# Strided and local attention into a gated two-layer MLP on one core: a planner with outstanding transfers, re-measured step lengths, and output weights behind the first attention units

## The chip, the cores and the metric

The kernel runs on one core of one Trainium2 chip. The time is device microseconds of one execution. The kernel before was timed in three runs: 538.31, 539.55 and 541.49 us, median 539.55. One more execution, 537.99 us long, was taken with a profile; all rows of the trace come from it.

## What is computed

Eight batches of eight heads, 576 tokens each, head width 64. The first four heads see a local window of 32 tokens, the other four see the tokens of their own residue modulo 32. The attention output, 4608 tokens by 512, goes through a first product with `w_in` (512 by 1024), a softmax gate, a layer norm with gain `g_ln`, and a second product with `w_out` (1024 by 512).

```python
scores = scale * np.matmul(q, k.transpose(0, 1, 3, 2))
mask_local = (rel >= 0) & (rel < stride)
mask_strided = (rel >= 0) & (pos[None, :] % stride == pos[:, None] % stride)
...
attn = attn / (np.sum(attn, axis=-1, keepdims=True) + 1e-09)
x = np.ascontiguousarray(attn_out.transpose(0, 2, 1, 3)).reshape(B * S, H * D)
h = x @ w_in
solu = h * softmax(h)
ln = (solu - mu) / np.sqrt(var + 1e-06) * g_ln
return (ln @ w_out).astype(np.float32)
```

(`softmax` stands here for the four lines of the reference that write it out.)

## The kernel before

**Two kinds of work.** An attention *unit* is a part of a batch: units 0 and 1 of a batch are the strided heads (12 and 10 blocks of 54), units 2, 3 and 4 the local heads (6 times 2 blocks of 96, three blocks of 64 queries each). There are 40 units. A *tile* is 128 tokens of the MLP; there are 36, and `ff(n)` writes tile n.

**A unit** (function `unit`) multiplies q and k on PE into `s_ps` (lines 381 and 386), takes the maximum and subtracts it on DVE (392, 393), the exponential on ACT (395), the sum and its reciprocal on DVE (396, 400, 401), the product with the reciprocal on POOL (404), splits the result into two fp16 parts on ACT (410) and DVE (411), and transposes them by DMA from SP (413). PE then multiplies with v into `x_ps` (434), and ACT (450) and DVE (451) split the result into the ring `xhi`, `xlo`. A strided unit uses both banks of `x_ps`, so the next unit's product waits for lines 450 and 451. The v of a batch is scaled and split (343), and copies of it are moved within the core by DMA (line 357: four into `vd` for the strided heads, three into `ve` for the local ones); line 434 waits for these moves as well.

**A tile** has a first product of two halves, 12 matmuls of 128x512 each, into two of the three banks of `h_ps` (492 to 494), a maximum on DVE (499, 500), exp on ACT (501), the gated product on DVE (503, 506), a square on ACT (507), small norms on POOL (511 to 545), the fp16 split on ACT (552) and DVE (553), one transpose by DMA (556; for the last two tiles four smaller ones, 560), the second product of two halves, 12 matmuls each (565 to 567), and a store from ACT (573 and the DMA behind it). The banks rotate, so the first half of tile n+1 goes into a bank that tile n doesn't use, and its second half waits for line 503 of tile n.

**The weights.** `w_in` (four loads of 1 MB) and `w_out` (four loads of 1 MB) come as 64-bit floats and are decoded by ACT (593) and DVE (596, 597). For `w_in` follow squares on ACT (606), a sum on PE (284), a power-of-two scale on DVE (290 to 296), and the split into two parts (611 on ACT, 612 on DVE). For `w_out` follow squares (622), eight matmuls of fp32 (632) with a matrix of gains that POOL writes (627), a scale, and the folding of gain and mean into the weights (641, 645, 647, 648). The sum of the squares of `w_out` uses a bank of `h_ps` that the first product of tile 0 needs.

**What sets the order.** Nothing is scheduled at run time. Each step is given to a `Plan` with its engine, a length, what it reads and writes, and for some a due time: `G1[n]` for the first product of tile n, `G2[n]` for its second, `PV[n]` for a unit's product with v. `dues` hands due times back from a step to those that it depends on, with a slack factor for each engine. `order` then plays the program through, always taking, on the engine that is free first, the ready step with the earliest due time, and the kernel is written out in that order. Each engine runs its instructions in that order and waits where a result is missing. The order of steps on the same buffers is that in which they were given to the plan. In `Plan` before, a DMA takes a fixed latency of 5.34 on top of its length, and a transpose from SP is a DMA like any other.

**The DMA queue.** SP issues nearly all DMAs, in order; the stores come from ACT. Eight semaphores are handed out in turn to the DMAs, so a DMA isn't issued before the eighth DMA ahead of it has landed.

Of the kernel before, what the change touches and what calls it, by code (L numbers as in the profile page):

```python
# [18 lines left out]
STRIDE = 32  # L19
# [41 lines left out]
class Plan:  # L61

    DMA_LATENCY = 5.34
    DMA_AHEAD = 1.0
    HOP = 0.50
    SLACK = {"pe": 0.89, "act": 1.59, "dve": 1.94, "pool": 0.82, "sp": 0.80}
    LOAD_LEAD = 6.88  # L70

    def __init__(self):
        self.steps = []
        self.dma = {}
        self.loads = set()
        self.writer, self.readers = {}, {}

    def add(self, eng, dur, fn, key, r=(), w=(), lock=None, dma=None):
        n = len(self.steps)
        if dma:  # L80
            self.dma[n] = dma
# [14 lines left out]
        self.steps.append((eng, dur, fn, key, deps, lock))  # L96

    def dues(self):
        steps = self.steps
        due = self.due = [float("inf") if s[3] is None else s[3] for s in steps]  # L100
        for m in range(len(steps) - 1, -1, -1):
            for d in steps[m][4]:
                e, dur = steps[d][:2]
                need = due[m] - dur * self.SLACK[e] - self.HOP
                if e == "sp":
                    need -= self.DMA_LATENCY
                if d in self.dma:
                    need -= self.dma[d] + self.DMA_LATENCY
                if not steps[d][4] or d in self.loads:
                    need -= self.LOAD_LEAD  # L110
                due[d] = min(due[d], need)

    def order(self):
        steps = self.steps
        self.dues()
        key = self.due
# [8 lines left out]
        dma_free = 0.0  # L125
# [5 lines left out]
        while len(out) < len(steps):  # L131
            best = None
            for e, ns in waiting.items():
# [3 lines left out]
                n = min((n for n in ns if ready_at[n] <= now), key=lambda n: (key[n], n))  # L137
# [6 lines left out]
            if e == "sp":  # L144
                dma_free = max(dma_free, now + 0.55) + dur
                free[e] = max(now + 0.55, dma_free - self.DMA_AHEAD)
                end = dma_free + self.DMA_LATENCY
            elif n in self.dma:
                free[e] = now + dur
                dma_free = max(dma_free, free[e]) + self.dma[n]  # L150
                end = dma_free + self.DMA_LATENCY
            else:
                if steps[n][5]:
                    now = max(now, locked["pool" if e == "dve" else "dve"])
                    locked[e] = now + dur
                free[e] = end = now + dur
# [10 lines left out]
def attn_solu_kernel(ctx: ExitStack, tc: tile.TileContext, qloc, qstr, kloc, kstr, vloc, vstr, w_in, w_out, g, masks, out):  # L167
# [107 lines left out]
    def pow2_scale(dst, parts, r, w, room, top=14, mul=1.0, square=None):  # L275
# [24 lines left out]
        add("dve", 0.2, root, None, r=[T], w=[(w, "root")])  # L300
        add("dve", 0.5, fn, None, r=[(w, "root")], w=[w])
# [5 lines left out]
    def load_qk(b, half):  # L307
        w = 2 * (S, SP)[half]
        k0 = 0 if half else KPAD
        load(1.65, q_raw[half][:, 0:w], (qloc, qstr)[half][b], [("q", half)])  # L310
        load(1.65, k_raw[half][:, k0 : k0 + w], (kloc, kstr)[half][b], [("k", half)])


    def load_v(b, a):
        w = [("vr", a, raw_v(b))] + ([("room", i) for i in range(4)] + [("half", i) for i in range(8)] if b == 2 else [])
        load((1.8, 2.2)[a], vr_sb[raw_v(b)][a], (vloc, vstr)[a][b], w)

    def v_scale(b):
# [43 lines left out]
    def unit(n):  # L362
# [29 lines left out]
        add("dve", w + 0.13, lambda: nc.vector.tensor_reduce(mx.rearrange("p (c x) -> p c x", c=2), sv, axis=AX.X, op=ALU.max), None, r=SS, w=[M])
        add("dve", w + 0.13, lambda: nc.vector.tensor_tensor(t4, sv, mx.rearrange("p (c x) -> p c x", c=2).unsqueeze(3).broadcast_to([P, 2, nb, nk]), op=ALU.subtract),
            None, r=[*SS, M], w=[T])
        add("act", nx * nk / 1200 + 0.19, lambda: nc.scalar.activation(tv, tv, AF.Exp, scale=0.125), None, r=[T], w=[T])
        add("dve", w + 0.1, lambda: nc.vector.tensor_reduce(sm, tv, axis=AX.X, op=ALU.add), None, r=[T], w=[M])
# [7 lines left out]
        add("pool", nx * nk / 500 + 0.1, lambda: nc.gpsimd.tensor_tensor(tv, tv, sm.unsqueeze(2).broadcast_to([P, nx, nk]), op=ALU.mult),  # L404
# [6 lines left out]
        add("dve", w + 0.1, lambda: nc.vector.tensor_tensor(lo, tv, hi, op=ALU.subtract), None, r=[T, PB], w=[PB], lock=True)  # L411
        nt = nx if half else 2 * nx
        add("sp", 0.16 * nt, lambda: nc.sync.dma_start_transpose(ptb[:, 0:nt], pb[:, 0:nt].rearrange("p a k -> p (a k)")), None, r=[PB], w=[PT])
# [24 lines left out]
        add("pe", nx * (0.063 if half else 0.095) + 0.1, pv, PV[n], r=[PT, *VR], w=X)  # L438
# [16 lines left out]
    def ff(n):  # L455
# [21 lines left out]
        else:  # L477
# [8 lines left out]
            add("dve", 0.3, cross, None, r=[(x, b % 4) for b in bs for x in ("hsc", "osc")], w=SC, lock=True)  # L486
# [12 lines left out]
        add("dve", 1.21, lambda: nc.vector.tensor_reduce(nm, hv, axis=AX.XY, op=ALU.max, negate=True), None, r=HH, w=[(ST, "nm")])  # L499
# [3 lines left out]
        add("dve", 1.3, lambda: nc.vector.scalar_tensor_tensor(uv, hv, 1.0, ev, op0=ALU.mult, op1=ALU.mult, accum_out=us), None,  # L503
# [3 lines left out]
        add("act", 1.35, lambda: nc.scalar.activation(e, u, AF.Square, bias=mean, scale=Q, accum_out=sq), None,  # L507
# [6 lines left out]
        if n < EARLY:  # L514
# [6 lines left out]
            add("pool", 1.0, first, None, r=[(ST, "mean"), (ST, "sq"), "nhalf"], w=[(ST, "r")], lock=False)  # L521
# [223 lines left out]
```

## Time and profile before

| | |
|---|---|
| median of three runs (lowest to highest) | 539.55 us (538.31 to 541.49) |
| profiled execution: its time, and the span of its trace | 537.99 us, 536.3 us |
| busy time of PE, DVE, ACT, POOL | 473.2, 363.0, 298.4, 172.1 us |
| mean granted clock of TensorE | 0.978 |

The page gives for each engine the time in which it ran an instruction. A row of the timeline has the start, the length, the engine, the line, the operation with its tiles and shapes, and, in brackets, how long the engine had been idle and what let it go. A row of the windows has a stretch of the span, and for PE, PEld, DVE, ACT and POOL the busy time and number of instructions in it, then the granted TensorE clock, the mean busy share of the 16 DMA engines (sums over queues can pass 1) and GB/s. A row of the waits has the total, the count and the longest.

### The profile page before, as it was taken

How to read it: one execution, taken by the hardware profiler on the slowest of the kernel's cores; microseconds unless marked ns; L12 is line 12 of the kernel's file. 1: busy time of each engine (PE TensorE's matmuls, PEld its weight loads, DVE VectorE, ACT ScalarE, POOL GpSimd, SP SyncE). 2: the span in 40 equal slices, each digit the busy share in tenths (PEclk: the TensorE clock that was granted, in tenths of full speed). 3: DMA queues.
4: the chain of work that ended last, by engine and by line, in shares of the span. 5: the costliest groups of instructions: out<-in, count | busy, mean ns of one | idle time of the engine just before them, and what ended most of it. 6: DMA issues, size and time to landing. Idle time of an engine off the chain costs nothing.

```text
span 536.3 us, 11679 instructions
## 1 busy us (share of the span) xinstructions
PE 473.2 (88%) x4780; PEld 242.5 (45%) x4780; DVE 363.0 (68%) x627; ACT 298.4 (56%) x432; POOL 172.1 (32%) x314
## 2 busy tenths in 40 slices
PE   2027848899999999998999999999999999999994
PEld 2013524445454555554545454455555454444441
DVE  2977896779676767685767676796667766645440
ACT  3857563487566556654665557555456554543541
POOL 3123005265232443332443222233234423321220
PEclk9998888799999999999999999999999999999999
DMA  8999884999995999599956995699746974443332
GB/s 343 370 223 355 169 227 121 168 147 274 258 215 101 279 193 213 119 195 257 223 111 180 198 255 111 125 240 195 165 90 141 224 160 89 90 88 78 81 85 72
DMA packets 155349, 96.89 MB, mean 181 GB/s; under 512 B 138272, under 2 KB 138912, under 8 KB 154784
## 3 DMA queue, kind: packets, MB, share of 16 engines
q1 hardware_dynamic: 150112, 86.71, 74.0%
q10 hardware_dynamic: 5184, 9.44, 5.3%
q8 instruction: 37, 0.61, 0.5%
q14 instruction: 16, 0.13, 0.1%
HBM read 39.24 MB, written 9.44 MB: 91 GB/s over the span
## 4 chain that ended last, share of the span: by engine, by line
PE 73%; DMA 13%; DVE 7%; POOL 2%; issue 2%; ACT 2%; SPq 1%; ACTq 0%; POOLq 0%; DVEq 0%
PE h_ps L492 10%; PE o_ps L565 10%; PE h_ps L493 10%; PE h_ps L494 10%; PE o_ps L567 10%; PE o_ps L566 10%; DMA cc<-cc 7%; PE x_ps L434 5%; PE s_ps L386 4%; DMA raw<-w_out 3%; DMA pt<-p 2%; DMA vrs<-vstr 1%; PE s_ps L381 1%; PE o_ps L632 1%; DVE st L499 1%
## 5 line engine op out<-in xcount | busy, mean ns | idle before, releaser
L492 PE MATMUL h_ps<-w,xhi 128*128 128x512 f16 x280 | 108.0, 386 | 1.3 <-DVE raw L503 1.2
L493 PE MATMUL h_ps<-w,xhi 128*128 128x512 f16 x280 | 107.9, 385 | 0.0
L494 PE MATMUL h_ps<-w,xlo 128*128 128x512 f16 x280 | 107.8, 385 | 0.0
L565 PE MATMUL o_ps<-obuf,cc 128*128 128x512 f16 x272 | 103.4, 380 | 3.6 <-DMA cc<-cc 3.6
L566 PE MATMUL o_ps<-obuf,cc 128*128 128x512 f16 x272 | 103.1, 379 | 0.0
L567 PE MATMUL o_ps<-obuf,cc 128*128 128x512 f16 x272 | 103.1, 379 | 0.0
L404 POOL TENSOR_TENSOR t<-t,m 128x576 f32<-128x576 f32 (+2 forms) x40 | 54.7, 1368 | 92.8 <-DVE m L401 34.9
L499 DVE TENSOR_REDUCE st<-h_ps 128x1 f32<-128x1024 f32 x35 | 42.7, 1221 | 53.4 <-PE h_ps L494 51.8
L533 POOL TENSOR_SCALAR st<-st 128x1 f32<-128x1 f32 x32 | 10.5, 327 | 175.5 <-DVE st L506 175.1
L553 DVE SCALAR_TENSOR_TENSOR cc<-raw,st,cc 128x1024 f16<-128x1024 f32 (+1 forms) x38 | 48.9, 1290 | 17.5 <-ACT cc L552 17.5
L501 ACT ACTIVATE raw<-h_ps,st,vsc 128x1024 f32<-128x1024 f32 x31 | 37.3, 1203 | 39.5 <-DVE st L500 39.1
L552 ACT ACTIVATE cc<-raw,st 128x1024 f16<-128x1024 f32 (+1 forms) x38 | 41.6, 1100 | 23.9 <-POOL st L542 19.7
L507 ACT ACTIVATE raw<-raw,st 128x1024 f32<-128x1024 f32 x36 | 41.3, 1147 | 18.8 <-DVE st L506 12.9
L411 DVE TENSOR_TENSOR p<-t,p 128x576 f16<-128x576 f32 (+2 forms) x40 | 30.4, 759 | 25.2 <-ACT p L410 25.2
L503 DVE SCALAR_TENSOR_TENSOR raw<-h_ps,raw 128x1024 f32<-128x1024 f32 x35 | 42.5, 1215 | 6.3 <-ACT raw L501 6.3
L567 PEld LDWEIGHTS <-cc 128*128 128x128 f16 x288 | 28.1, 98 | 37.1 <-DMA cc<-cc 3.2
L565 PEld LDWEIGHTS <-cc 128*128 128x128 f16 x288 | 28.1, 97 | 36.7 <-DMA cc<-cc 4.9
L494 PEld LDWEIGHTS <-xlo 128*128 128x128 f16 x288 | 28.5, 99 | 35.1 <-issue 1.9
L493 PEld LDWEIGHTS <-xhi 128*128 128x128 f16 x288 | 28.5, 99 | 34.4 <-issue 3.4
L492 PEld LDWEIGHTS <-xhi 128*128 128x128 f16 x288 | 28.5, 99 | 34.0 <-issue 1.9
L386 PE MATMUL s_ps<-k,q 64*54 64x54 f32 (+1 forms) x1280 | 41.8, 274 | 1.8 <-DMA k<-kstr 1.8
L573 ACT ACTIVATE ob<-o_ps,st 128x512 f32<-128x512 f32 x34 | 23.3, 684 | 35.3 <-PE o_ps L567 30.8
(130 smaller groups left out, 727.2 us busy)
## 6 DMA issues: line engine op xcount, KB each, us to landing
out<-ob ACTq DMA_DIRECT2D x36, 256.0 KB, 3.1
vd<-vs SPq DMA_DIRECT2D x16, 384.0 KB, 6.2
q<-qstr SPq DMA_DIRECT2D x8, 594.0 KB, 4.6
k<-kstr SPq DMA_DIRECT2D x8, 594.0 KB, 5.6
q<-qloc SPq DMA_DIRECT2D x8, 576.0 KB, 5.2
k<-kloc SPq DMA_DIRECT2D x8, 576.0 KB, 6.5
raw<-w_in SPq DMA_DIRECT2D x4, 1024.0 KB, 12.5
vrs<-vstr SPq DMA_DIRECT2D x5, 768.0 KB, 7.8
```

The lines of the kernel that those rows point to most:

```text
L386: nc.tensor.matmul(s_ps[row : row + nq, pair, i * nk : (i + 1) * nk], q_raw[half][hs, q0 : q0 + (nq - 1) * nqb + 1 : nqb], k_raw[half][hs, ...
L404: add("pool", nx * nk / 500 + 0.1, lambda: nc.gpsimd.tensor_tensor(tv, tv, sm.unsqueeze(2).broadcast_to([P, nx, nk]), op=ALU.mult), None, ...
L492: nc.tensor.matmul(hv[:, i], xhi[:, cc, tok], whi[:, cc, cols], start=(cc == 0), stop=False)
L493: nc.tensor.matmul(hv[:, i], xhi[:, cc, tok], wlo[:, cc, cols], start=False, stop=False)
L494: nc.tensor.matmul(hv[:, i], xlo[:, cc, tok], whi[:, cc, cols], start=False, stop=(cc == 3))
L499: add("dve", 1.21, lambda: nc.vector.tensor_reduce(nm, hv, axis=AX.XY, op=ALU.max, negate=True), None, r=HH, w=[(ST, "nm")])
L503: add("dve", 1.3, lambda: nc.vector.scalar_tensor_tensor(uv, hv, 1.0, ev, op0=ALU.mult, op1=ALU.mult, accum_out=us), None, r=[*HH, E], w=[ ...
L552: add("act", w / 1020 + 0.15, lambda cols=cols: nc.scalar.mul(c[:, 0, cols], u[:, cols], r), None, r=[U, (ST, "r")], w=CC[0][mine])
L553: add("dve", w / 880 + 0.15, lambda cols=cols: nc.vector.scalar_tensor_tensor(c[:, 1, cols], u[:, cols], r, c[:, 0, cols], op0=ALU.mult, o ...
L565: nc.tensor.matmul(o, ct[:, cc, :], ohi[:, cc, :], start=(cc == 0), stop=False)
L566: nc.tensor.matmul(o, ct[:, cc, :], olo[:, cc, :], start=False, stop=False)
L567: nc.tensor.matmul(o, ct[:, 8 + cc, :], ohi[:, cc, :], start=False, stop=(cc == 7))
```

## The change

It changes the planner, its numbers, and the place of two groups of steps. No instruction is added or removed, and none changes its shape.

- The planner knows eight outstanding transfers (`lanes`), a landing time (`LAND`, `LATE`), and for each SP step how long the issuing engine is held (`issue=(took, hold)`): a transpose holds SP until shortly before it lands. Locks between DVE and POOL are applied to all steps.
- Nearly all step lengths, the slack factors and the due times have new numbers. `LAG`, the planned distance between a tile's first and second product, went from 31.30, 34.52, 17.64 (first tile, seventh tile, last tile) to 33.36, 47.73, 50.87.
- The first piece of `w_out` depends on the writer of the second transpose buffer (`("pt", 1)`). As the piece is given to the plan behind units 0 to 4, that writer is the transpose of unit 3.
- `prep_o()` (everything on `w_out`) is given to the plan behind the units of batch 0, not ahead of them; the factor that needs its result is a function of its own, `o_factor`.

```diff
-FIRST = 3.59
-STEP = 12.74
-LEAD = 18.32
-LAG = [31.30, 34.52, 17.64]
+FIRST = -1.35
+STEP = 12.91
+LEAD = 17.42
+LAG = [33.36, 47.73, 50.87]
...
-    DMA_LATENCY = 5.34
-    DMA_AHEAD = 1.0
-    HOP = 0.50
-    SLACK = {"pe": 0.89, "act": 1.59, "dve": 1.94, "pool": 0.82, "sp": 0.80}
-    LOAD_LEAD = 6.88
+    LAND = 2.3
+    LANES = 8
+    HOP = 0.21
+    LATE = 0.59
+    SLACK = {"pe": 1.49, "act": 1.44, "dve": 1.24, "pool": 2.53, "sp": 4.64}
+    LOAD_LEAD = 4.91
...
+            if steps[n][5]:
+                now = max(now, locked["pool" if e == "dve" else "dve"])
+                locked[e] = now + dur
+            if n in self.issue:
+                took, hold = self.issue[n]
+                if e != "sp":
+                    now += dur
+                now = max(now, lanes[lane])
+                dma_free = max(now + 0.8, dma_free) + (dur if e == "sp" else 0.5)
+                landed = lanes[lane] = dma_free + self.LAND - 0.8
+                lane = (lane + 1) % self.LANES
+                free[e] = now + took if hold is None else max(now + took, landed - hold)
+                end = landed + self.LATE
...
+    def o_factor(b):
+        sc = vsc_sb[b % 4]
         add("dve", 0.2, lambda: nc.vector.tensor_scalar(sc[:, 3:4], sc[:, 4:5], ...
...
-        add("sp", 0.16 * nt, lambda: nc.sync.dma_start_transpose(...), None, r=[PB], w=[PT])
+        add("sp", 0.142 * nt, lambda: nc.sync.dma_start_transpose(...), None, r=[PB], w=[PT], issue=(1.0, 3.5))
...
-        load(2.9, room, src, RAW)
+        load(2.61, room, src, RAW, [("pt", 1)] if n == 4 else [])
...
     prep_w()
-    prep_o()
...
+            if b:
+                o_factor(b + 1)
         unit(b * NU + NU - 1)
+        if b == 0:
+            prep_o()
+            o_factor(0)
+            o_factor(1)
```

What this makes of the order is shown here on three engines. In these rows the number behind `m`, `t` and `p` counts the buffer: in batch 0, `m0` to `m4` belong to units 0 to 4, and `p0`, `p1`, `p2`, `p0`, `p1` to units 0 to 4 in turn. Line numbers of the changed kernel are 4 lower in `unit`, `ff` and the weights (6 lower in the first functions).

DVE at the start, around the scale of `w_in` (`w_sc`), before:

```order
L343 SCALAR_TENSOR_TENSOR vl0_71<-vrl0_69,vsc0_77,vl0_71 128x1280
L596 TENSOR_SCALAR raw0_67<-raw0_67 128x1024
L597 SCALAR_TENSOR_TENSOR obuf0_113<-obuf0_113,raw0_67 128x1024
L396 TENSOR_REDUCE m1_90<-t1_86 128x10
L290 TENSOR_SCALAR w_sc0_114<-h_ps_119 128x1
```

and now:

```order
L592 TENSOR_SCALAR raw0_67<-raw0_67 128x1024
L593 SCALAR_TENSOR_TENSOR cc0_101<-cc0_101,raw0_67 128x1024
L447 TENSOR_TENSOR xlo0_100<-x_ps_120,xhi0_99 128x2x18x18
L407 TENSOR_TENSOR p0_94<-t3_88,p0_94 128x6x96
L339 SCALAR_TENSOR_TENSOR vl0_71<-vrl0_69,vsc0_77,vl0_71 128x1280
L284 TENSOR_SCALAR w_sc0_114<-h_ps_119 128x1
```

Ahead of the scale stood the decoding of the first piece of `w_out` (into `obuf`) and unit 1's sum; now the result of unit 0 (`xlo`, line 447) and unit 3's split stand there, and the decoding of `w_out` has moved behind.

SP at the start (`raw` and `cc` are loads of weights, `q1`, `k1`, `vr` loads of batch 1, `vd` and `ve` moves of v, `pt` the transposes), before:

```order
L305 DMA raw0_67<-w_out 128x2x1024
L357 DMA vd0_74<-vs0_72 64x2x1536 x2
L357 DMA vd0_74<-vs0_72 64x1536 x2
L305 DMA vrs0_70<-vstr 128x1536
L657 DMA g0_116<-g 128x8
L305 DMA q10_64<-qstr 128x1188
L413 DMA_TRANSPOSE pt0_97<-p0_94 128x12x128
L305 DMA vrl0_69<-vloc 128x1280
L305 DMA raw0_67<-w_out 128x2x1024 x2
```

and now:

```order
L299 DMA q10_64<-qstr 128x1188
L299 DMA k10_66<-kstr 128x1188
L409 DMA_TRANSPOSE pt0_97<-p0_94 128x12x128
L353 DMA vd0_74<-vs0_72 64x2x1536 x2
L409 DMA_TRANSPOSE pt1_98<-p1_95 128x10x128
L353 DMA vd0_74<-vs0_72 64x1536 x2
L299 DMA vrs0_70<-vstr 128x1536
L299 DMA raw0_67<-w_out 128x2x1024
L409 DMA_TRANSPOSE pt1_98<-p0_94 128x12x128
```

Unit 0's transpose had one piece of `w_out` and the four moves into `vd` ahead of it; now it has neither, and two of the moves stand behind unit 1's transpose.

ACT at the end (a row of 569 or 573 is the store of a tile; `st0` to `st3` are tiles 32 to 35 here, and the row that reads `x_ps` is the exponential of the last tile), before:

```order
L501 ACTIVATE raw0_67,st3_107<-x_ps_120,st3_107,vsc3_80 128x1024
L507 ACTIVATE raw0_67,st3_107<-raw0_67,st3_107 128x1024
L573 ACTIVATE ob1_103<-o_ps_121,st1_105 128x512
L574 DMA out<-ob1_103 128x512
L552 ACTIVATE cc0_101<-raw0_67,st3_107 128x512 x2
L573 ACTIVATE ob0_102<-s_ps_118,st2_106 128x512
L574 DMA out<-ob0_102 128x512
L573 ACTIVATE ob1_103<-s_ps_118,st3_107 128x512
```

and now:

```order
L497 ACTIVATE raw0_67,st3_107<-x_ps_120,st3_107,vsc3_80 128x1024
L503 ACTIVATE raw0_67,st3_107<-raw0_67,st3_107 128x1024
L569 ACTIVATE ob0_102<-o_ps_121,st0_104 128x512
L570 DMA out<-ob0_102 128x512
L548 ACTIVATE cc0_101<-raw0_67,st3_107 128x512 x2
L569 ACTIVATE ob0_102<-s_ps_118,st2_106 128x512
L570 DMA out<-ob0_102 128x512
L569 ACTIVATE ob1_103<-o_ps_121,st1_105 128x512
L570 DMA out<-ob1_103 128x512
L569 ACTIVATE ob1_103<-s_ps_118,st3_107 128x512
```

Behind the exponential of the last tile stood the stores of tiles 33, 34 and 35; now those of 32, 34, 33 and 35 stand there.

More of the change, by code (lines that the diff above doesn't have):

```diff
@@ L95, in add @@
         lock = eng == "pool" if lock is None else lock
-        self.steps.append((eng, dur, fn, key, deps, lock))
+        self.steps.append((eng, dur, fn, due, deps, lock))
+        if issue or eng == "sp":
+            self.issue[n] = issue or (0.45, None)
     def dues(self):
@@ L115, in order @@
         self.dues()
-        key = self.due
+        due = self.due
         left = [len(s[4]) for s in steps]
@@ L136, in order @@
                 now = max(free[e], min(ready_at[n] for n in ns))
-                n = min((n for n in ns if ready_at[n] <= now), key=lambda n: (key[n], n))
+                n = min((n for n in ns if ready_at[n] <= now), key=lambda n: (due[n], n))
                 if best is None or now < best[0]:
@@ L254, in load_masks @@
     def load_masks():
-        add("sp", 0.6, lambda: nc.sync.dma_start(mask_sb, masks), None, w=["mask_raw"])
-        add("pool", 1.5, masks_bf16, None, r=["mask_raw"], w=["mask"])
+        add("sp", 0.4, lambda: nc.sync.dma_start(mask_sb, masks), None, w=["mask_raw"])
+        add("pool", 1.34, masks_bf16, None, r=["mask_raw"], w=["mask"])
     for i in range(NPB):
@@ L348, in v_split @@
             moves = (
-                (1.3, ve_sb[0:D], v_sb[0][D:P]),
-                (0.5, ve_sb[D:KL, :, 0:last], v_sb[0][0:STRIDE, :, cd:]),
-                (0.1, ve_sb[D:KL, :, last:], v_sb[0][0:STRIDE, :, 0:cd]),
-            )
-        else:
-            moves = [(1.2, vd_sb[0:D, :, y], v_sb[1][y * D : y * D + D]) for y in range(2)]
-            moves += [(0.6, vd_sb[D:P, 0, y], v_sb[1][y * D : y * D + D, 0]) for y in range(2)]
+                (1.0, ve_sb[0:D], v_sb[0][D:P]),
+                (0.4, ve_sb[D:KL, :, 0:last], v_sb[0][0:STRIDE, :, cd:]),
+                (0.2, ve_sb[D:KL, :, last:], v_sb[0][0:STRIDE, :, 0:cd]),
+            )
+        else:
+            moves = [(1.0, vd_sb[0:D, :, y], v_sb[1][y * D : y * D + D]) for y in range(2)]
+            moves += [(0.4, vd_sb[D:P, 0, y], v_sb[1][y * D : y * D + D, 0]) for y in range(2)]
         for i, (dur, dst, src) in enumerate(moves):
@@ L519, in first @@
                 nc.gpsimd.tensor_tensor(r, v, nhalf, op=ALU.pow)
-            add("pool", 1.0, first, None, r=[(ST, "mean"), (ST, "sq"), "nhalf"], w=[(ST, "r")], lock=False)
+            add("pool", 1.9, first, None, r=[(ST, "mean"), (ST, "sq"), "nhalf"], w=[(ST, "r")], lock=False)
             def second():
@@ L569, in ff @@
         for i in range(2):
-            add("pe", 2.6, lambda i=i: g2(i), G2[n], r=[(*CT, i, 0), (*CT, i, 1), *(("o_w", cc) for cc in range(4 * i, 4 * i + 4))], w=[O])
+            add("pe", 2.62, lambda i=i: g2(i), G2[n], r=[(*CT, i, 0), (*CT, i, 1), *(("o_w", cc) for cc in range(4 * i, 4 * i + 4))], w=[O])
         def store():
@@ L627, in gains @@
             nc.gpsimd.tensor_scalar(gmat, g_sb.unsqueeze(2).broadcast_to([P, 8, P]), -1.0 / DF, None, op0=ALU.mult)
-        add("pool", 2.3, gains, None, r=["g"], w=["gmat"])
+        add("pool", 2.8, gains, None, r=["g"], w=["gmat"])
         for cc in range(8):
-            add("pe", 0.87, lambda cc=cc: nc.tensor.matmul(o_ps, gmat[:, cc], obuf[:, cc], start=(cc == 0), stop=(cc == 7)), None,
+            add("pe", 1.0, lambda cc=cc: nc.tensor.matmul(o_ps, gmat[:, cc], obuf[:, cc], start=(cc == 0), stop=(cc == 7)), None,
                 r=["gmat", ("od", cc)], w=["o"])
```

118 lines of the change are left out of this document (50 added, 68 removed).

## The prediction

> **What bounds the kernel now.** I read the page first, then windows that cut the span where PE changes its pace, then the timelines of PE and DVE at the start and at the end. The page has PE busy for most of the span, and its slices show where it isn't: in the first seven and in the last.
>
> ```profile
> PE 473.2 (88%) x4780; PEld 242.5 (45%) x4780; DVE 363.0 (68%) x627; ACT 298.4 (56%) x432; POOL 172.1 (32%) x314
> ...
> PE   2027848899999999998999999999999999999994
> ...
> PEclk9998888799999999999999999999999999999999
> ```
>
> The windows put numbers on it (first number after the stretch: its length; next: PE busy; third of the busy times: DVE).
>
> ```profile
> 0.00:20.00 20.00, 3.72 (x98) 3.03 (x98) 9.48 (x18) 11.26 (x12) 7.56 (x18) 1.00 0.91 367
> 20.00:40.00 20.00, 3.03 (x60) 2.42 (x60) 16.21 (x26) 13.63 (x21) 2.49 (x1) 1.00 1.08 256
> 40.00:60.00 20.00, 14.13 (x182) 7.64 (x183) 16.97 (x25) 13.86 (x26) 4.90 (x4) 0.87 1.10 318
> 60.00:80.00 20.00, 11.96 (x174) 6.78 (x176) 17.37 (x35) 11.29 (x18) 2.42 (x2) 0.84 0.80 182
> 80.00:97.70 17.70, 13.77 (x167) 7.57 (x161) 13.04 (x24) 7.28 (x10) 6.78 (x4) 0.79 0.57 116
> 97.70:134.00 36.30, 35.12 (x361) 17.90 (x361) 29.36 (x58) 24.49 (x36) 19.39 (x33) 0.93 0.97 209
> 134.00:500.00 366.00, 362.27 (x3620) 184.39 (x3619) 251.00 (x433) 203.67 (x292) 121.42 (x234) 1.00 0.80 169
> 500.00:536.30 36.30, 29.15 (x134) 12.78 (x132) 9.59 (x15) 12.93 (x20) 7.11 (x20) 1.00 0.32 80
> ```
>
> PE's idle time is length less busy time: 16.3 + 17.0 + 5.9 + 8.0 + 3.9 = 51.1 us up to 97.7, 1.2 us from there to 134, 3.7 us in the long middle, 7.2 us at the end. From 97.7 to 500 PE is the bound at 99%, and an order can gain there at most those 4.9 us. The change must pay at the start and at the end. At the start DVE is busy for 64 us of the 77.7 from 20 to 97.7, and the DMA engines hardly rest (0.91, 1.08, 1.10, 0.80): all weights, two batches of q, k and v, and the first units meet there.
>
> **The start.** PE stops waiting at 97.73, with the second half of tile 2's first product, let go by DVE's line 503 of tile 1 (0.08 us of accumulator read stand behind the second row).
>
> ```profile
> 8.69 0.83 DVE L392 TENSOR_REDUCE m<-s_ps 128x12 f32<-128x648 f32 x1 [7.59 <-PE s_ps L386]
> ...
> 80.40 4.89 DVE L648 TENSOR_TENSOR obuf<-raw,obuf 128x512 f16<-128x512 f32 x8
> ...
> 91.58 1.23 DVE L499 TENSOR_REDUCE st<-h_ps 128x1 f32<-128x1024 f32 x1 [4.60 <-PE h_ps L494]
> ...
> 96.46 1.21 DVE L503 SCALAR_TENSOR_TENSOR raw<-h_ps,raw 128x1024 f32<-128x1024 f32 x1
> ...
> 8.69:91.58 82.89, 42.38 (x540) 23.68 (x540) 66.73 (x110) 53.37 (x81) 19.24 (x11) 0.90 0.94 261
> ...
> 97.73 0.58 PE L492 MATMUL h_ps<-w,xhi 128*128 128x512 f16 x1 [1.19 <-DVE raw L503]
> ```
>
> From its first maximum at 8.69 to tile 1's maximum at 91.58, DVE works 66.7 of 82.9 us; 16.2 us are gaps. The changed order has nearly the same DVE steps ahead of tile 1's maximum (tile 0's line 553 more, 1.3 us; one maximum of 0.7 less). So the start moves by what happens to these 16.2 us, and I count the gaps of the new order.
>
> (1) The first unit's sum now stands ahead of the second unit's maximum. The sum waits for ACT's exponential:
>
> ```profile
> 9.56 0.83 DVE L393 TENSOR_TENSOR t<-s_ps,m 128x648 f32<-128x648 f32 x1
> ...
> 12.02 0.72 ACT L395 ACTIVATE t<-t 128x648 f32<-128x648 f32 x1
> ```
>
> DVE is idle from 10.4 to 12.7, 2.3 us, where before it did another maximum.
>
> (2) DVE's row `xlo` of unit 0 now stands ahead of the scale of `w_in`, as the first order view shows, so it holds up all four lines 612. It needs unit 0's transpose, all four moves into `vd`, line 434 on PE and line 450 on ACT. Before, these came at:
>
> ```profile
> 30.77 5.22 SPq L413 DMA_TRANSPOSE pt<-p  x1
> ...
> vd<-vs SPq DMA_DIRECT2D x2, 384.0 KB, 14.3
> ...
> vd<-vs SPq DMA_DIRECT2D x2, 192.0 KB, 15.2
> ...
> 42.36 1.48 PE L434 MATMUL x_ps<-pt,vd 118*64 118x54 f16 x48
> ...
> 44.62 0.83 DVE L451 TENSOR_TENSOR xlo<-x_ps,xhi 128x648 f16<-128x648 f32 x1 [0.17 <-ACT xhi L450]
> ```
>
> (The latencies are those of the first 54 us.) In the middle of the kernel, with less queued, they are:
>
> ```profile
> vd<-vs SPq DMA_DIRECT2D x12, 384.0 KB, 6.2
> ...
> pt<-p SPq DMA_TRANSPOSE x33, 4.7
> ```
>
> Now the transpose is issued when unit 0's split is done, near 18 by adding the DVE steps ahead of it. In the queue then lie these three kinds and the like:
>
> ```profile
> q<-qstr SPq DMA_DIRECT2D x8, 594.0 KB, 4.6
> ...
> raw<-w_in SPq DMA_DIRECT2D x4, 1024.0 KB, 12.5
> ...
> vrs<-vstr SPq DMA_DIRECT2D x5, 768.0 KB, 7.8
> ```
>
> Strided q and k twice (4 x 594 KB), v (768 and 640), masks (144), local q and k (2 x 576) and `w_in` (4 x 1024) make 9.2 thousand KB, 9.4 MB; at the first window's 367 GB/s they are through near 25. One transpose takes it to about 30 (4.7), the moves behind it to about 33, unit 1's transpose and the last two moves to 36 or 37; PE and ACT then take 2.3 us as before (42.36 to 44.62). So I put unit 0's `xlo` at 39. The DVE steps ahead of it, in the new order, end near 34. The gap is 5 us; its ends are 0 (moves land by 31) and 13 (the latencies of the first 54 us apply to the moves again, 32 + 15, then 2.3: above 47).
>
> (3) The scale of `w_out` waits for a sum on PE that is now followed without a break by half of tile 1's first product. Such a wait ended late before: tile 1's maximum at 91.58 needed 24 matmuls, but was let go only when the third half had ended, too.
>
> ```profile
> 88.14 0.38 PE L492 MATMUL h_ps<-w,xhi 128*128 128x512 f16 x1
> 88.36 0.38 PE L493 MATMUL h_ps<-w,xhi 128*128 128x512 f16 x1
> ...
> 91.17 0.38 PE L494 MATMUL h_ps<-w,xlo 128*128 128x512 f16 x1
> ```
>
> Half a product is 12 x 0.215 = 2.6 us, less some 1 us of unit 6's maximum and subtraction that stand in the gap: 1.6 us.
>
> (4) Tile 0's line 553 now stands right behind the eight lines 648. It needs POOL's norms, which the eight lock out, and ACT's line 552:
>
> ```profile
> 80.58 4.84 POOL L517 TENSOR_SCALAR st<-st 128x1 f32<-128x1 f32 x1 [12.24 <-DVE st L506]
> ...
> 86.50 1.15 ACT L552 ACTIVATE cc<-raw,st 128x1024 f16<-128x1024 f32 x1 [2.94 <-POOL st L519]
> ```
>
> The eight ended at 85.3 and ACT at 87.65: a gap of 2.3 us that unit 7's maximum and the wait for PE covered.
>
> (5) Loads that come late for the decoding of `w_out`, which before left its own gaps: 1.5 us, a guess between 0 and 4.
>
> Together 2.3 + 5 + 1.6 + 2.3 + 1.5 = 12.7 against 16.2 us; less 0.6 of added work and 0.3 for the mask, which is loaded third rather than first, tile 1's maximum comes 2.6 us earlier. About 1 us of this I take off again, because the first half of tile 0's second product, now ahead of tile 2's second half, must wait for a transpose issued only then. **Start: 1.6 us gained, between a loss of 7 and a gain of 7.** So the head start of the units is mostly spent by DVE's in-order queue.
>
> The clock is a second matter here. Matmuls start every 0.22 us at 88.14, but:
>
> ```profile
> 82.11 0.63 PE L493 MATMUL h_ps<-w,xhi 128*128 128x512 f16 x1
> 82.54 0.63 PE L494 MATMUL h_ps<-w,xlo 128*128 128x512 f16 x1
> ```
>
> 0.43 us at 82.11; the first matmul at 97.73 is as slow (0.58), and the granted clock from 97.7 to 134 is 0.93. That stretch is PE-bound, so 0.07 x 36.3 = 2.5 us are lost there. I expect the same loss again, as PE again comes out of short gaps: no term. The Trainium skill, "TensorE: Matmul & The Clock Gate", section "Part 1: The HAM clock gate (the "warmup" mystery)", says that the clock is halved after an idle window of about 3.4 us; the 0.43 and 0.22 agree with halving, but the gap ahead of 97.73 is only 1.19 us. By that rule a start without long gaps would keep the full clock, and the sum would be 2.5 us lower.
>
> **The middle.** Of the waits on PE, one is that of the second product for its transposes:
>
> ```profile
> PE o_ps L565 <- DMA cc<-cc: 3.6, 3, 1.7
> ```
>
> With `LAG` near 50, a tile's second product stands behind the first product of three further tiles rather than two. That is one tile, some 12 us, more time for the transpose, so these 3.6 us go. New waits I put at 1 us (bounds 0 and 4): POOL, DVE and SP run other orders, and no row shows them. **Middle: 2.6 us gained (0 to 4.5).**
>
> **The end.** Before, after the last first product PE had the second products of tiles 33, 34 and 35 left. It waited twice:
>
> ```profile
> 513.11 0.38 PE L565 MATMUL o_ps<-obuf,cc 128*128 128x512 f16 x1
> ...
> 524.41 0.38 PE L565 MATMUL s_ps<-obuf,cc 128*128 128x512 f16 x1 [0.78 <-ACT ob L573]
> ...
> 527.69 0.39 PE L567 MATMUL s_ps<-obuf,cc 128*128 128x512 f16 x1 [2.69 <-DMA cc<-cc]
> ```
>
> The last tile's chain from its first product to its transposed pieces takes 527.69 - 513.11 = 14.6 us. PE had 48 matmuls for it, 48 x 0.215 = 10.3 us, and then waited 0.8 + 2.7. Now four tiles are left (stores 32, 34, 33, 35 in the last order view): 72 x 0.215 = 15.5 us, which covers the 14.6. The matmuls are the same in total, so the whole 3.5 us go. What is late next is only the store behind the last matmul, which stays. If the cover is short (ACT's store of tile 32 ahead of the last split, 0.7 us), 0.8 us come back. **End: 3.5 us gained (2.5 to 4).**
>
> **The sum.** 1.6 + 2.6 + 3.5 = 7.7 us from the profiled execution's 537.99 (1.7 us of which lie around its span of 536.3): 530.3. That execution lies 1.56 us below the median of the three runs shown; added, the forecast is 531.9 us.
>
> **The rivals.**
> *The start closes.* If the moves land by 34 or so, `xlo` waits for nothing; gaps (2) and (5) fall away, and half of (3) and (4): some 6 to 9 us more, 523 to 526 us. For it speaks that unit 0's transpose loses 1.2 MB of moves and 1 MB of `w_out` ahead of it. Against it speaks the DMA share near 1 in the first 60 us: the same bytes must go through.
> *The clock stays full.* If PE comes to tile 2 without the gaps of 0.8 to 2 us that stood there, the 2.5 us of slow clock fall away: 529.4 us. The slow rows behind short gaps speak against it.
> *No change.* The start loses what end and middle gain: `xlo` at 45, near where it stood (44.62): 531.9 + 6 = 538 us. For it speaks that the order of DVE around tiles 0 and 1 is almost the same.
> *Slower: the queue in front of DVE.* Each transpose holds SP (5.22 us in the row above), two transposes now stand among the moves, and moves that were issued into a full queue took 14.3 and 15.2 us. If they do so again, the last two moves, issued near 32, land at 47; with unit 1's transpose held up alike (unit 0's was issued at 30.77, and its product came at 42.36) line 434 comes at 49 to 52, and `xlo` at 51 to 54, 12 to 15 us later than I count. DVE stands still ahead of all of `w_in`'s split, and nothing later makes it up: 531.9 + 12 to 15 = 544 to 547 us. It decides from line 434 at 47 on: 10.4 us late, it takes the 7.7 and 2.7 more, the bound named below. Against it: the queue holds no `w_out` at that time.
>
> **How the numbers follow.** Forecast (529.5 to 536): 0.40. Full clock as well (529.4, counted with faster): 0.10. Start closes: 0.20. No change (537 to 542): 0.20. Slower: 0.10. About 0.5% (2.7 us) is what a measurement of this kernel can tell from no change. Faster by over that: 0.40 + 0.10 + 0.20 = 0.70; within: 0.20; slower: 0.10. The range takes the forecast, the full clock, the closed start, and half of no change: 523 to 540 us.
>
> **What would show it.** In the changed profile: the first matmuls of unit 0 with v near 36 to 37 (31 for the closed start, 47 and later for the slow rival), and behind them a DVE gap ended by `xlo` or ACT's `xhi`; tile 1's maximum near 89; PE without waits from about 96; no row of line 561 waiting for `cc` in the middle; no wait for `cc` at the last tile, and 96 matmuls between the last first product and the end. I am wrong if the start gains more than 7 us, or if PE shows waits of more than 4 us in the middle.

## The result and the profile after

The changed kernel takes 543.29 us (median of 20 runs, 539.64 to 548.17), the kernel before 538.09 us (20 runs, 532.07 to 543.30). The ratio is 1.0114, 95% interval 1.0083 to 1.0145: about 6 us slower, where 531.9 us were forecast. The profiled execution of the changed kernel took 548.17 us, the longest of the 20 and the only one of them counted as slow, which the ratio leaves out; a second profile (`after_again`, below) shows the same waits.

The page of the changed kernel, PE and its clock in 40 slices:

```profile
PE   2222966988899899996999989999999999999997
...
PEclk9999997899899999998999989999999999999999
```

PE has its first full slice earlier. But from 137 us on (a slice is 13.7 us, and ten lie ahead of it), where before all slices were full but one with an 8 and the last, one now has a 6 and three have an 8. The windows, with the cuts of the prediction:

```profile
0.00:20.00 20.00, 4.83 (x126) 4.16 (x126) 8.34 (x20) 9.00 (x11) 7.72 (x19) 1.00 0.92 370
20.00:40.00 20.00, 3.94 (x109) 3.44 (x111) 14.57 (x19) 11.76 (x17) 4.42 (x2) 1.00 1.06 288
40.00:60.00 20.00, 8.25 (x129) 5.16 (x124) 17.48 (x28) 17.17 (x26) 1.15 (x1) 1.00 0.99 288
60.00:80.00 20.00, 17.63 (x216) 9.52 (x215) 16.48 (x32) 10.43 (x21) 2.42 (x2) 1.00 0.88 227
80.00:97.70 17.70, 11.21 (x103) 5.42 (x103) 15.80 (x29) 9.31 (x15) 5.95 (x5) 0.76 0.55 119
97.70:134.00 36.30, 34.19 (x364) 17.50 (x363) 28.38 (x58) 24.81 (x36) 16.61 (x32) 0.98 0.88 189
134.00:500.00 366.00, 352.62 (x3552) 179.64 (x3550) 246.97 (x428) 199.91 (x287) 123.45 (x234) 0.99 0.78 166
500.00:546.50 46.50, 42.76 (x199) 19.17 (x196) 13.22 (x21) 15.20 (x23) 7.36 (x21) 1.00 0.32 80
```

Length less PE busy, summed to 97.7: 51.8 us idle, against 51.1 before. From 134 to 500 it is 366 - 352.62 = 13.4 us, against 3.7. Behind 500 it is 3.7, against 7.2: the end won 3.4 us. So the loss lies in the middle, where I had put a gain. PE's timeline there, with the waits in brackets (`pt` is a unit's transposed result, `cc` a tile's):

```profile
137.03 0.28 PE L430 MATMUL x_ps<-pt,ve 96*64 96x64 f16 x6 [1.68 <-DMA pt<-p]
146.53 0.39 PE L561 MATMUL o_ps<-obuf,cc 128*128 128x512 f16 x1 [1.67 <-DMA cc<-cc]
...
190.49 0.38 PE L488 MATMUL h_ps<-w,xhi 128*128 128x512 f16 x1 [1.40 <-DVE raw L499]
194.16 0.28 PE L430 MATMUL x_ps<-pt,ve 96*64 96x64 f16 x6 [0.92 <-DMA pt<-p]
252.66 0.28 PE L430 MATMUL x_ps<-pt,ve 96*64 96x64 f16 x6 [4.66 <-DMA pt<-p]
315.69 0.28 PE L430 MATMUL x_ps<-pt,ve 96*64 96x64 f16 x6 [2.31 <-DMA pt<-p]
```

By the order of steps on PE, the four rows of line 430 are the products with v of units 9, 14, 19 and 24, each the last unit of its batch. For unit 19, DVE's split and SP's queue:

```profile
235.57 0.75 DVE L407 TENSOR_TENSOR p<-t,p 128x576 f16<-128x576 f32 x1
```

```profile
232.05 4.66 SPq L353 DMA_DIRECT2D vd<-vs  x4
236.75 0.59 SPq L299 DMA_DIRECT2D raw<-vstr  x1
237.44 8.15 SPq L552 DMA_TRANSPOSE cc<-cc  x1
245.69 6.33 SPq L409 DMA_TRANSPOSE pt<-p  x2
```

The split is ready at 236.3. Ahead of its transpose SP issues the load of a later batch's v and tile 11's transpose, which holds SP for 8.15 us behind four moves and a load. The unit's transpose is issued at 245.69, 9.4 us after its data were ready.

At units 9, 14 and 24 only the four moves and the load stand ahead. There SP issues the transpose at 129.46, 184.81 and 306.36, 1.4 to 3.7 us after DVE's split, but the product with v starts 7.6 to 9.3 us after the issue; the median from issue to landing of all `pt` between 120 and 320 us is 4.5 us. So at these three the landing is late rather than the issue.

### The profile page after: what moved, and what is told of

Its sections match the earlier page's. It is cut to its first block, busy times and chain, and to the rows that moved or that the text cites. A ratio compares the mean times of both kernels' runs of the same rounds, so it can differ in the third digit from the quotient of the medians.

```text
span 546.5 us, 11685 instructions
## 1 busy us (share of the span) xinstructions
PE 475.4 (87%) x4780; PEld 244.0 (45%) x4780; DVE 361.2 (66%) x627; ACT 297.6 (54%) x432; POOL 169.1 (31%) x314
## 4 chain that ended last, share of the span: by engine, by line
PE 75%; DMA 10%; DVE 8%; ACT 2%; issue 2%; SPq 1%; POOL 0%; ACTq 0%; DVEq 0%; POOLq 0%
PE o_ps L561 11%; PE o_ps L562 10%; PE o_ps L563 10%; PE h_ps L488 10%; PE h_ps L490 10%; PE h_ps L489 10%; DMA pt<-p 5%; PE s_ps L382 5%; PE x_ps L430 5%; PE o_ps L628 2%; DMA cc<-cc 2%; DMA vrs<-vstr 1%; PE s_ps L377 1%; DMA raw<-w_out 1%; DVE raw L641 1%
## 5 line engine op out<-in xcount | busy, mean ns | idle before, releaser
L561 PE MATMUL o_ps<-obuf,cc 128*128 128x512 f16 x272 | 105.8, 389 | 1.7 <-DMA cc<-cc 1.7
L400 POOL TENSOR_TENSOR t<-t,m 128x576 f32<-128x576 f32 (+2 forms) x40 | 50.4, 1261 | 179.8 <-DVE m L397 140.7
L562 PE MATMUL o_ps<-obuf,cc 128*128 128x512 f16 x272 | 105.6, 388 | 0.0
L563 PE MATMUL o_ps<-obuf,cc 128*128 128x512 f16 x272 | 105.4, 387 | 0.0
L549 DVE SCALAR_TENSOR_TENSOR cc<-raw,st,cc 128x1024 f16<-128x1024 f32 (+1 forms) x38 | 47.0, 1241 | 24.1 <-ACT cc L548 24.1
L563 PEld LDWEIGHTS <-cc 128*128 128x128 f16 x288 | 28.7, 100 | 35.5 <-issue 2.7
L561 PEld LDWEIGHTS <-cc 128*128 128x128 f16 x288 | 28.6, 99 | 34.8 <-issue 2.5
L562 PEld LDWEIGHTS <-cc 128*128 128x128 f16 x288 | 28.7, 100 | 31.4 <-issue 2.5
```

The costliest lines, as they stand in the source:

```text
L400: add("pool", nx * nk / 520 + 0.03, lambda: nc.gpsimd.tensor_tensor(tv, tv, sm.unsqueeze(2).broadcast_to([P, nx, nk]), op=ALU.mult), None, ...
L549: add("dve", w / 980 + 0.23, lambda cols=cols: nc.vector.scalar_tensor_tensor(c[:, 1, cols], u[:, cols], r, c[:, 0, cols], op0=ALU.mult, o ...
L561: nc.tensor.matmul(o, ct[:, cc, :], ohi[:, cc, :], start=(cc == 0), stop=False)
L562: nc.tensor.matmul(o, ct[:, cc, :], olo[:, cc, :], start=False, stop=False)
L563: nc.tensor.matmul(o, ct[:, 8 + cc, :], ohi[:, cc, :], start=False, stop=(cc == 7))
```

## Experiments

The first theory (Q): SP's queue makes the unit's product with v wait. Its rival (D): PE is slowed by the orders of DVE and ACT, and the transposes only show it. Others (M, S, L, W, P) are stated where they come in. Most experiments give the changed kernel's steps in another order, written out as a list:

```diff
-    for n in plan.order():
+    for n in ORDER:
         plan.steps[n][2]()
```

**Which stretch loses.** Three kernels splice the two orders, at the first product of tile 3 and at that of tile 31.

> The changed order up to the first product of tile 3, the order of before from there to the end. Theory M (the loss lies in the middle, the start is even): the start's own loss is 0 to 1 us and nothing else is changed, so the ratio to before is 0.997 to 1.003. Rival S (the start loses, and the waits in the middle of the changed kernel's profile are particular to that long execution): 1.010 to 1.018, since the end's gain of 3.4 us is taken away from the measured loss of 6 us and more is then left.

> The order of before up to the first product of tile 3, the changed order from there to the first product of tile 31, the order of before for the end. Theory M: the middle alone loses the measured 6 us and the 3.4 us that the end gives back, so 8 to 10 us, ratio 1.013 to 1.020, with waits of line 430 for pt at units 9, 14, 19 and 24. Rival S: 1.000 to 1.004, and hardly any waits there.

> The order of before up to the first product of tile 31, the changed order from there. Both theories: the end's waits of 3.5 us go, ratio 0.992 to 0.995. If the end's gain needs the longer distance between the two products through the whole kernel, 0.998 to 1.002.

Measured: `h_start` 0.994 (0.9913 to 0.9966), `h_mid` 1.0157 (1.012 to 1.0194), `h_tail` 1.0083 (1.0057 to 1.0108). Theory S falls: the start alone gains 3.2 us, the middle alone loses 8.5, and its trace has waits of 5.6 us at the four units (one of them put down to DVE). The tail was a miss. By my reading the seam took cover away, which no run tests; PE waits where the changed order takes over:

```profile
471.32 0.37 PE L430 MATMUL x_ps<-pt,ve 96*64 96x64 f16 x6 [4.46 <-DMA pt<-p]
473.78 0.59 PE L488 MATMUL h_ps<-w,xhi 128*128 128x512 f16 x1 [1.29 <-DVE raw L499]
```

So a splice says nothing about an end alone; that is asked again below. `h_start` in windows (this execution, 531.67 us, is the fastest of its twelve):

```profile
0.00:97.70 97.70, 47.28 (x678) 28.68 (x679) 74.34 (x127) 59.19 (x89) 21.91 (x30) 0.95 0.88 263
97.70:134.00 36.30, 34.90 (x372) 18.02 (x371) 29.71 (x60) 24.96 (x38) 19.36 (x35) 1.00 0.94 206
134.00:500.00 366.00, 365.54 (x3636) 186.01 (x3635) 252.67 (x432) 205.19 (x295) 124.37 (x236) 1.00 0.77 167
```

With the changed start the old middle idles 0.5 us. PE's idle time up to 97.7 is 50.4 us (51.1 before), and the clock from 97.7 to 134 is 1.00 (0.93 before).

**Is it SP?** Three orders touch SP alone. The first moves the transposes of the last units of six batches; here unit 19's:

```diff
+L409 DMA_TRANSPOSE pt<-p
 L353 DMA vd<-vs x4
 L299 DMA raw<-vstr
 L552 DMA_TRANSPOSE cc<-cc
-L409 DMA_TRANSPOSE pt<-p
```

> The changed kernel, but on SP the transpose of the last unit of each batch (units 9, 14, 19, 24, 29, 34) stands ahead of the four moves of v, the load of v and the tile's transpose that stood ahead of it. Theory Q (SP's queue makes the unit's product with v wait in the middle): the four waits of line 430 for pt, 1.7 + 0.9 + 4.7 + 2.3 = 9.6 us in the profile, shrink to 0 to 3 us, and the time falls 5 to 9 us, to a ratio of 0.994 to 1.002. Rival D (PE is slowed by DVE and ACT, whose orders are coupled more tightly; the transposes only show it): the time stays within 2 us of the changed kernel's, 1.008 to 1.014, and waits for DVE or ACT take the place of those for pt.

> The changed kernel on PE, DVE, ACT and POOL, step for step; only SP issues its DMAs, from tile 3 on, in the order that the kernel before has there. Theory Q (SP's queue makes the middle's waits): the waits for pt at units 9, 14, 19 and 24 shrink to 0 to 3 us in all and the time falls by 5 to 9 us, to a ratio of 0.993 to 1.002. Theory D (the orders of PE, DVE and ACT make them, and SP only passes them on): it stays at 1.008 to 1.015.

> The converse: the changed start with the order of before behind it (the kernel that measured 0.994), but SP issues its DMAs in the changed order throughout. Theory Q: the middle's loss of 9 us comes back, 1.007 to 1.015. Theory D: 0.991 to 0.998, as without it.

Measured: `units_first` 1.0308 (1.0272 to 1.0345), `sp_before` 1.1165 (1.1121 to 1.1208), `sp_changed` 1.1114 (1.1082 to 1.1146). All three missed both theories. `units_first` on SP, and then on PE, around unit 9:

```profile
117.97 4.63 SPq L552 DMA_TRANSPOSE cc<-cc  x1
126.63 2.56 SPq L409 DMA_TRANSPOSE pt<-p  x1
129.24 4.52 SPq L353 DMA_DIRECT2D vd<-vs  x4
```

```profile
144.86 1.09 PE L430 MATMUL x_ps<-pt,vd 118*64 118x54 f16 x48 [3.52 <-DMA pt<-p]
150.89 0.61 PE L561 MATMUL o_ps<-obuf,cc 128*128 128x512 f16 x1 [4.94 <-DMA cc<-cc]
...
233.50 0.32 PE L377 MATMUL s_ps<-mk_loc,unit 64*64 64x288 bf16 x4 [2.67 <-DVE vsc L284]
```

SP stands still from 122.6 to 126.6 for unit 9's split, the moves and loads behind it are late, and the next unit, the next tile and the scale of v wait. In the wholesale exchanges SP waits for results that the other engines bring in another order; `sp_before`:

```profile
SPq L552 <- DVE cc L549: 166.6, 23, 16.6
SPq L409 <- DVE p L407: 36.3, 10, 10.2
```

One engine's order can't be taken into another plan. These runs didn't decide between Q and D; a smaller edit was needed.

**The distance between the two products, and the two halves of the change.** `lag_only` and `lag_tail` move second products on PE and their copies on ACT; `place_only` and `planner_only` each undo one half of the diff shown above. `lag_tail` on PE, from tile 30 on:

```diff
-ff30 L561
 ff33 L488
 ff34 L488
+ff30 L561
-ff31 L561 x2
 ff34 L488
 ff35 L488
+ff31 L561 x2
-ff32 L561 x2
 ff35 L488
+ff32 L561 x2
 ff33 L561 x2
```

> The changed start with the order of before behind it, and one thing more: each tile's second product, with its copy out and store, stands one tile later on PE and ACT from tile 1 on; SP, DVE and POOL are untouched. Theory L (the longer distance itself does harm: it brings every first product and every product with v 5.2 us of PE work closer to DVE, ACT and SP, so that the units' transposes come late): waits for pt in the middle of 3 to 8 us, ratio 0.997 to 1.006. Theory Q or D: the middle stays free of waits and the end gains its 3.3 us, 0.985 to 0.990.

> The changed start with the order of before behind it, and the second product of a tile one tile later only from the second half of tile 30 on, behind the last unit's product with v, so that four tiles are left after the last first product. All theories: the waits of 0.8 and 2.5 us at the end go, 0.986 to 0.990. If the first products that move up by 5.2 us there wait for DVE's line 499 instead, 0.992 to 0.996.

> One part of the change alone: the planner and all its numbers as before, but everything on w_out is given to the plan behind the units of batch 0, and its first piece waits for the second transpose buffer. If the start's gain comes from this placement, 0.990 to 0.996, with the middle free of waits as before. If the old numbers can't use the placement, 1.000 to 1.010.

> The other part alone: the changed planner and all its numbers, but w_out is given to the plan in its old place and waits for no transpose buffer. If the middle's loss of 9 us comes from the numbers (theories Q and D), it is still there, and the start's gain of 3 us is missing: 1.010 to 1.025. If the loss comes from the placement (a later w_out shifting everything), 0.992 to 1.003.

Measured: `lag_only` 0.995 (0.9926 to 0.9975), `lag_tail` 0.9969 (0.9943 to 0.9996), `place_only` 1.0106 (1.0061 to 1.015), `planner_only` 1.031 (1.0265 to 1.0355). `lag_only` lies just outside both of its expectations. Of the 3 to 8 us of waits for `pt` in the middle that L asked for, its trace has one of 2.4 us (at 421.82), so the longer distance doesn't make the middle's loss and L falls; but it gains nothing on `h_start` (0.994) either. `lag_tail` misses both of its ranges as well. Two new waits stand where the moved product had stood, and a third one waits for a store:

```profile
485.02 0.38 PE L488 MATMUL h_ps<-w,xhi 128*128 128x512 f16 x1 [0.94 <-DVE raw L499]
494.58 0.38 PE L488 MATMUL h_ps<-w,xhi 128*128 128x512 f16 x1 [1.63 <-DVE raw L499]
514.00 0.38 PE L561 MATMUL o_ps<-obuf,cc 128*128 128x512 f16 x1 [1.13 <-ACT ob L569]
```

They sum to 3.7 us, more than the wait of 2.5 us for `cc` that the end lost (the one of 0.8 us stayed). Of the change's two halves neither is faster by itself, and the numbers alone lose the most, more than either theory had allowed. The windows of these two place the loss. From 134 to 500 PE idles 13.0 us in `planner_only`, against 13.4 in the changed kernel, and 3.3 us in `place_only`, against 3.7 before: the middle's loss comes with the planner and its numbers, not with the place of `w_out`. What `place_only` loses lies ahead of 134, where PE idles 56.4 us (52.3 before) and the clock from 97.7 on is 0.86; how that comes about I did not take apart.

**Four places on SP, or on PE.** `sp_fix` leaves all other engines as they are and moves the transposes of units 9, 14, 19 and 24 past the load, unit 19's past the tile's transpose as well. For unit 19:

```diff
 L353 DMA vd<-vs x4
+L409 DMA_TRANSPOSE pt<-p
 L299 DMA raw<-vstr
 L552 DMA_TRANSPOSE cc<-cc
-L409 DMA_TRANSPOSE pt<-p
```

> The changed kernel, but on SP the transposes of units 9, 14, 19 and 24 stand ahead of the load of v (768 KB) that stood directly ahead of them, unit 19's also ahead of tile 11's transpose; the four moves of v stay ahead of them, so that SP comes to them no earlier than it did to the load. Theory Q (what is queued directly ahead of these transposes makes PE wait for pt): the waits of 1.7 + 0.9 + 4.7 + 2.3 us shrink to 0 to 3 us in all, the time falls by 4 to 8 us, ratio 0.995 to 1.003. Theory W (these waits are only where a lack of cover comes out; taken away here they come out at the next place): the time stays within 2 us of the changed kernel's, 1.007 to 1.014, with new waits at other lines.

`pv_later` instead moves line 430 of these units on PE:

```diff
-unit19 L430
 ff10 L561
 unit21 L382
 ff14 L488
+unit19 L430
```

> The changed kernel, but on PE the product with v of units 9, 14 and 24 stands half a tile's product (2.6 us) later, and that of unit 19 two halves (5.2 us) later, so that PE has work where it waited for pt. Theory P (PE was planned too early for these four units): the waits of 9.6 us shrink to 0 to 3 us and the time falls by 4 to 8 us, ratio 0.995 to 1.003. Theory W: within 2 us of the changed kernel's, 1.007 to 1.014.

Measured: `sp_fix` 534.96 us, 0.9946 (0.992 to 0.9972); `pv_later` 547.62 us, 1.018 (1.014 to 1.022). Theory Q holds, with a gain just past its range, and W falls here; so does D, as DVE and ACT keep the changed orders. Four transposes on SP are worth 1.0114 - 0.9946 = 0.0168, or 9.0 us, and PE's idle time from 134 to 500 falls from 13.4 to 5.8 us. Of the waits of line 430 for `pt` in `sp_fix` one is left, 4.5 us at the start:

```profile
PE x_ps L430 <- DMA pt<-p: 4.5, 1, 4.5
```

Its SP at unit 19:

```profile
230.82 4.28 SPq L353 DMA_DIRECT2D vd<-vs  x4
235.29 2.01 SPq L409 DMA_TRANSPOSE pt<-p  x1
237.35 1.18 SPq L299 DMA_DIRECT2D raw<-vstr  x1
238.58 5.05 SPq L552 DMA_TRANSPOSE cc<-cc  x1
```

The transpose is issued 10.4 us earlier, as soon as its data are ready (DVE's split ends at 235.26 here), and holds SP for 2.01 us, not as one of two in 6.33. Both P and W missed on `pv_later`. It is no faster than the changed kernel; that it is slower is not certain, as the two intervals just overlap (1.014 and 1.0145). The waits left line 430, as P said, but new ones came for DVE, 7.2 us for 9.6, as W said:

```profile
200.01 0.38 PE L488 MATMUL h_ps<-w,xhi 128*128 128x512 f16 x1 [1.59 <-DVE raw L499]
267.27 0.58 PE L488 MATMUL h_ps<-w,xhi 128*128 128x512 f16 x1 [3.44 <-DVE raw L499]
320.60 0.38 PE L488 MATMUL h_ps<-w,xhi 128*128 128x512 f16 x1 [2.19 <-DVE raw L499]
```

DVE had stood still ahead of unit 19's `xlo`, for ACT's `xhi`, and so for the product with v that PE now did later:

```profile
254.61 0.56 DVE L447 TENSOR_TENSOR xlo<-x_ps,xhi 128x384 f16<-128x384 f32 x1 [5.36 <-ACT xhi L446]
```

That all of the extra time comes from this was not tried.

**The rest.** Three more kernels ask whether the waits repeat, whether the wait for `cc` at 146.5 has the same cause, and whether the end's gain is real inside the changed order. `sp_fix2` has on SP, besides the four:

```diff
+L552 DMA_TRANSPOSE cc<-cc
 L299 DMA q<-qstr
 L299 DMA k<-kstr
-L552 DMA_TRANSPOSE cc<-cc
```

> The changed kernel once more, for a second profile, since the first profiled execution was a long one. Theory Q: the waits of line 430 for pt at units 9, 14, 19 and 24 are there again, 6 to 10 us in all. If they were particular to the first execution: under 3 us.

> The changed kernel with the four transposes ahead on SP (the one that measured 0.995), and one thing more on SP: tile 3's transpose stands ahead of the loads of q and k of batch 3 (2 x 594 KB), not behind them. If SP's queue makes the wait of 3.1 us for cc at 146.7 as well: that wait falls to 0 to 1 us and the ratio to 0.987 to 0.992. If the wait has another cause, 0.993 to 0.997.

> The kernel with the four transposes ahead on SP (0.995), but from tile 30 on the second product stands one tile earlier again on PE and ACT, so that three tiles are left after the last first product, as before the change. If the end's term was right (four tiles cover the last tile's chain and the gain is real): the waits of 0.8 and 2.5 to 2.7 us at the end are back, 0.999 to 1.003. If the cover at the end is paid for by waits at the place that it was taken from (as the kernel with only the last products moved showed): 0.993 to 0.997.

Measured: `after_again` 547.91 us in its one execution, `sp_fix2` 532.29 us, 0.9872 (0.9839 to 0.9905), `end_undone` 1.0008 (0.9975 to 1.0041). The second profile of the changed kernel:

```profile
144.91 0.60 PE L561 MATMUL o_ps<-obuf,cc 128*128 128x512 f16 x1 [2.33 <-DMA cc<-cc]
...
192.92 0.28 PE L430 MATMUL x_ps<-pt,ve 96*64 96x64 f16 x6 [1.30 <-DVE st L495]
251.52 0.37 PE L430 MATMUL x_ps<-pt,ve 96*64 96x64 f16 x6 [4.75 <-DMA pt<-p]
315.17 0.28 PE L430 MATMUL x_ps<-pt,ve 96*64 96x64 f16 x6 [1.67 <-DMA pt<-p]
```

With 0.90 us at unit 9 the four waits sum to 8.6 us: they repeat (two are put down to DVE in this trace, by the last event seen). In `sp_fix2` the wait for `cc` is gone as well, as expected of SP's queue: 0.9946 - 0.9872 = 0.0074, or 4.0 us for a wait of 3.1, which in `sp_fix` was followed by 3.4 us of slow matmuls. PE's idle time from 134 to 500 is down to 3.0 us, and the kernel is faster than both others. `end_undone` gives back 1.0008 - 0.9946 = 0.0062, or 3.3 us, and the two intervals don't overlap: inside the changed order the end's gain is real.

## Why the prediction was wrong

**The start: the size near, the way there wrong.** Line 430 of unit 0 came at 35.09 and 36.13 (36 to 37 predicted), held by the moves, and `xlo` at 38.27 behind a gap of 5.12 us on DVE (39 and 5 predicted); the loss from 47 on did not occur. But tile 1's maximum, which was to come 2.6 us earlier, stood where it had stood (91.58 before).

```profile
35.09 0.31 PE L430 MATMUL x_ps<-pt,vd 118*64 118x54 f16 x4 [11.98 <-DMA vd<-vs]
36.13 1.38 PE L430 MATMUL x_ps<-pt,vd 118*64 118x54 f16 x44 [0.72 <-DMA vd<-vs]
...
91.63 1.23 DVE L495 TENSOR_REDUCE st<-h_ps 128x1 f32<-128x1024 f32 x1 [1.73 <-PE h_ps L490]
```

In the eight traces whose order is the changed one up to tile 3 (the changed kernel twice, `h_start`, `lag_tail`, `sp_fix`, `sp_fix2`, `pv_later`, `end_undone`) it came at 89.71 to 92.13, in the three with the old start (before, `h_mid`, `h_tail`) at 90.84 to 91.58: 0.1 us earlier in the mean. Tile 2's maximum came at 100.95 to 104.00 against 104.72 to 105.52, 2.6 us earlier in the mean. So the measured gain of 3.2 us arose behind tile 1's maximum, and not from DVE's gaps ahead of it; that 1.6 us had been predicted is luck. The clock is part of it: "I expect the same loss again" was wrong, as from 97.7 to 134 it was 0.97 to 1.00 in the eight and 0.93 to 0.94 in the three. How much is the clock, and how much shorter waits, no run separates.

**The end: the size right, the reason incomplete.** 3.5 us were predicted and 3.3 measured, and the changed kernel's trace has neither of the two waits. But "The matmuls are the same in total, so the whole 3.5 us go" forgets that the delayed matmuls were cover where they stood. In `lag_tail` waits came back there.

**The middle: the step that failed.** "New waits I put at 1 us (bounds 0 and 4): POOL, DVE and SP run other orders, and no row shows them." By the runs the middle lost 6.1 + 3.2 + 3.3 = 12.6 us (result, start and end, if the three parts add up; `h_mid`, with the middle alone, lost 8.5), where 2.6 were to be gained. Five places on SP are worth 13.0 (1.0114 - 0.9872). Rows did bear on it: the prediction quotes a transpose that holds SP for 5.22 us and counts what lies ahead of unit 0's, but does so at the start alone. SP's order around each batch change would have shown the load ahead of the last unit's transpose, and at unit 19 a tile's transpose as well.

**Why bounds of 4 us were too small.** The four waits are 9.6 us by their brackets, and a wait can be followed by slow matmuls, so that more is lost than the wait. Behind the wait of 1.67 us at 146.53:

```profile
146.75 0.38 PE L562 MATMUL o_ps<-obuf,cc 128*128 128x512 f16 x1
...
147.20 0.63 PE L561 MATMUL o_ps<-obuf,cc 128*128 128x512 f16 x1
147.63 0.63 PE L562 MATMUL o_ps<-obuf,cc 128*128 128x512 f16 x1
...
150.60 0.38 PE L563 MATMUL o_ps<-obuf,cc 128*128 128x512 f16 x1
150.81 0.38 PE L488 MATMUL h_ps<-w,xhi 128*128 128x512 f16 x1
```

From 147.20 to 150.60 matmuls start every 0.43 us, then every 0.22: 1.7 us lost again. Behind the waits of 4.66 and 2.31 us they are as slow for 2.9 and 3.4 us; behind that of 1.68 us, at 137.03, they start every 0.22 us at once.

**The waits for `cc`:** in the changed kernel there is one wait of 1.7 us, and `sp_fix2` shows that it is at SP's hand. That the longer distance removed the 3.6 us is not shown: with the old distance in the middle these waits were 3.6 us in the trace before, 1.9 in `lag_tail`, 0.4 in `h_tail` and 0.3 in `h_start`. The term was read off one execution.

**The rivals.** The slower one named the right queue, SP's with transposes among moves, but put it at the start, in front of DVE, and asked for 10.4 us there.

## What to carry to other kernels

When an order changes, walk each in-order queue at every place where it repeats, and for each transpose ask what was issued just ahead of it and when its data are ready; here 9 us hung on four places in SP's order. In these runs such a transpose cost time both behind a load that was not needed yet and, in `units_first`, ahead of all else before its own data were there. Work moved to cover a wait can leave the place it came from bare, as in `lag_tail`: price that place too.

## What the hardware did that I had not expected

Tile 11's transpose held SP for 8.15 us behind four moves and a load of v, and for 5.05 us in `sp_fix`, where the unit's transpose stands between: its size alone does not set the hold. What in the queue does was not tried.

A wait of 1.67 us on PE was followed by a slow stretch of 3.4 us, one of 1.68 us by none, and in `end_undone` one of 2.08 us for the same `cc` by none. The Trainium skill, "TensorE: Matmul & The Clock Gate", section "Part 1: The HAM clock gate (the "warmup" mystery)", has the clock return after about 3.4 us of work; here the slow stretches behind these waits lasted 2.9 to 3.4 us, and the one from 97.73 in the trace before lasted 5.0. It has the clock fall after an idle window of about 3.4 us; here it fell behind some shorter waits and not behind others, and which of them do it these traces do not settle.
